# Six stores instead of five leave out one DMA engine, in 26 pieces each, and V gets a sixth buffer

## The chip, the cores and the metric

The kernel runs on one core of a Trainium2 chip. A core has five engines that work at the same time and meet through semaphores: TensorE (PE; its weight loads are listed as PEld), VectorE (DVE), ScalarE (ACT), GpSimd (POOL) and SyncE (SP). Sixteen DMA engines move data between the chip's main memory (DRAM) and the on-chip memory (SBUF, 128 partitions). Any of SP, ACT and POOL can issue a transfer; each has its own queue on every one of the sixteen engines.

The metric is the device time of one execution in microseconds (us). The kernel before takes 1285.98 us, the median of three runs (1284.94 to 1286.35).

## The reference

It is attention for one query row per head, with its gradients. There are 2 x 32 = 64 heads; each has a K and a V of 8192 rows by 128, in bfloat16.

```python
def _fwd_reference(q, k, v):
    scale = q.shape[-1] ** -0.5
    scores = jnp.einsum("bhqd,bhkd->bhqk", q, k) * scale
    p = _softmax(scores, axis=-1)
    return jnp.einsum("bhqk,bhkd->bhqd", p, v)

def reference(q, k, v, grad_out):
    ...
    _out, _vjp = jax.vjp(_f, q, k, v)
    _grads = _vjp(grad_out)
    ...
    return (_out0, *[jnp.asarray(_g) for _g in _grads])
```

So the kernel returns the output (64 x 128), the gradient of q (64 x 128), and the gradients of K and V, which are as large as K and V: 64 x 8192 x 128 each. K and V are 268 MB together and are read once; their gradients are 268 MB and are written once. The gradient of K is, in each head, an outer product of a column of weights `dS` with the row q, that of V an outer product of the weights `P` with the row of grad_out.

## The kernel before

**Tiles.** One K or V of a head is a tile of 128 partitions x 64 x 128 (2 MB, 16 KB in each partition). `load(h)` takes one buffer `kt` and one `vt` from a pool of `UNITS = 5` each and has SP load K and then V (L104). The gradients are written over K and V in the same buffers: `outer` (L271, DVE) puts the gradient of V into `vt` and that of K into `kt`, and `store` (L331, ACT) writes a buffer out. A buffer is free for the next load when its store has landed.

**Stages.** An iteration `h` of the main loop has eight steps `j`, each in two halves. PE transposes K (`j` 0 to 3) and V (`j` 4 to 7) of head `h` by a product with the identity (L113); ACT, in two places DVE, copies the result out of PSUM (`ev`, L120 and L118); PE multiplies it by the column of q or grad_out (L136). Beside it the head before, `p = h - 1`, is finished: sums, weights, the products with `rows` (L241), and the eight `outer`. The V gradient of `p` is stored at `j = 4`, the K gradient at `j = 7`; both issues stand in ACT's instruction stream among its copies. At the end of iteration `h`, `load(h + 3)` is issued by SP. Heads 0 to 4 are loaded at the start. The last head's two gradients are stored in halves.

**The order around the change.** The order on each engine is written out (`manual_schedule`); waits are put in by the framework. Two of its habits matter. First, the transfers of SP and ACT take turns on eight semaphores, in the order of the program, and the transfers of POOL on another eight: a transfer waits on its issuing engine until the one eight places earlier has landed. In an ordinary head four transfers of SP and ACT are issued (store V, store K, load K, load V), so that each waits for its own kind of two heads earlier. Secondly, a pool hands out its buffers in the order in which the planner expects them to be free, not strictly in turn.

**The stores in pieces.** `store` hands every 26th of the 128 gradients (`(2 * h + w) % RARE == RARE // 2 - 1`; `w` 0 is V, 1 is K) to `store_by_fifteen`. Those are numbers 12, 38, 64, 90 and 116: the V gradients of heads 6, 19, 32, 45 and 58. `store_by_fifteen` writes the 128 partitions in 24 pieces (L299) with POOL, not ACT. Partitions 16 to 19 and 48 to 51, which the code calls `fifth`, go out in four pieces of two. Between the pieces stand 11 transfers `turn(n)` (L285): four bytes twice from each of `n` rows of q, into a tile `spare` that nobody reads. Pieces and turns are laid in such an order that, as the function's name says, fifteen of the sixteen DMA engines carry the data. So POOL issues 35 transfers for one such store, and ACT none. The pieces of four partitions with `size=16384` go out as rows of 16 KB, the others as two packets of 8 KB a row.

Of the kernel before, what the change touches and what calls it, by code (L numbers as in the profile page):

```python
# [11 lines left out]
BF16 = mybir.dt.bfloat16  # L12
# [3 lines left out]
HC = CH // 2  # L16
QG = 4
OG = 4
RARE = 26
UNITS = 5  # L20


@with_exitstack
def kernel(
# [11 lines left out]
    nc = tc.nc  # L36
    B, H, Sq, D = q.shape
    Sk = k.shape[2]
    P = nc.NUM_PARTITIONS
    assert Sq == 1 and D == P  # L40
    BH = B * H
    NT = Sk // P
# [5 lines left out]
    const = ctx.enter_context(tc.tile_pool(name="const", bufs=1))  # L48
# [17 lines left out]

    kvp = ctx.enter_context(tc.tile_pool(name="kv", bufs=UNITS))
    evp = ctx.enter_context(tc.tile_pool(name="ev", bufs=5))
# [28 lines left out]
    def load(h):  # L97
        x = heads[h]
        x.kv = [
            kvp.tile([P, NT, D], BF16, name="kt", tag="kt"),  # L100
            kvp.tile([P, NT, D], BF16, name="vt", tag="vt"),
        ]
        for dst, src in zip(x.kv, (k_v, v_v)):
            nc.sync.dma_start(out=dst[:], in_=src[h])  # L104
# [173 lines left out]
    turns = []  # L278

    def turn(n):  # L280

        i = 4 * len(turns)
        turns.append(n)
        two = lambda t: t.rearrange("p (a b) -> p a b", a=2)
        nc.gpsimd.dma_start(  # L285
            out=two(spare[0:n, :])[:, :, i : i + 2], in_=two(q_rows[0:n, :])[:, :, 0:2]
        )

    def store_by_fifteen(h, w):

        dst, src = (dv_v, dk_v)[w][h], heads[h].kv[1 - w]

        def rows(lo, n, step=4, size=8192):
            own = slice(lo, lo + step * (n - 1) + 1, step)
            nc.gpsimd.dma_start(out=dst[own], in_=src[own], max_dma_last_dim=size)  # L299

        def fifth(r):
            rows(16 + r, 2, step=32)

        for r in range(4):

            if r == 1:
                fifth(r)
                turn(14)
            rows(52 + r, 11)
            rows(r, 4, size=16384)  # L310
            if r == 0:
                fifth(r)
                turn(3)
            elif r == 3:
                turn(10)
                fifth(r)
                turn(9)
            else:
                turn(5)
            rows(20 + r, 3)  # L320
            if r == 2:
                fifth(r)
                turn(14)
            rows(96 + r, 8)
            rows(32 + r, 4, size=16384)
            turn(5)

    def store(h, w, a=0, b=NT):
        if (2 * h + w) % RARE == RARE // 2 - 1:
            return store_by_fifteen(h, w)  # L330
        nc.scalar.dma_start(out=(dv_v, dk_v)[w][h][:, a:b, :], in_=heads[h].kv[1 - w][:, a:b, :])  # L331

    def outer_and_store(h, w, i):

        outer(h, w, i)
        if h == BH - 1 and i % 2:
            store(h, w, (i - 1) * CH, (i + 1) * CH)


    spare = const.tile([16, 1024], BF16)  # L340
    turn(5)
    nat = const.tile([BH, 2, D], BF16)
    for i, src in enumerate((q_rows, do_rows)):
# [9 lines left out]
    with tc.manual_schedule():  # L353
        for h in range(min(UNITS, BH)):
            load(h)
        for h in range(BH + 1):
# [4 lines left out]
            for j in range(NS):  # L361
# [24 lines left out]
                if x and p < BH - 1 and j in (4, 7):  # L386
                    store(p, j // 7)
# [7 lines left out]
                if j == 7:  # L395
                    if x and UNITS <= h + 3 < BH:
                        load(h + 3)
                    if y and h % QG == 0:
                        spread_rows(h // QG)
        for w, dst in enumerate((o_rows, dq_rows)):  # L400
            tps = ps_tp.tile([BH, P], BF16, name="tps", tag="tp")
            nc.tensor.transpose(tps[:], colsT[:, w, :], ident_bf[:])
            rows = const.tile([BH, D], BF16, name=f"rows{w}")
# [33 lines left out]
```

## Time and profile before

| | us |
|---|---|
| median of three runs (1284.94 to 1286.35) | 1285.98 |
| the profiled execution | 1286.92 |
| its span, first to last instruction | 1285.1 |
| PE, ACT, DVE busy | 1060.3, 909.3, 883.8 |
| POOL busy | 105.8 |

The profile is of one execution. Its page gives the busy time of each engine, then the span in 40 equal slices of 32 us (busy tenths of each engine, the share that the DMA engines were busy, and the GB/s that they moved), the DMA queues, and groups of instructions with what ended the idle time ahead of them. In these views, q1 is SP's queue (loads), q10 is ACT's (stores), q0 is POOL's (the pieces and turns), and q8 fetches instructions. The trace holds more than the views print: a record of every DMA packet, with its queue, start, duration and size, but not the number of the engine that moved it.

| packets of | size | count | usual ns of one |
|---|---|---|---|
| loads, q1 | 16 KB | 16384 | 611 |
| stores, q10 | 16 KB | 15488 | 611 |
| pieces, q0 | 16 KB | 160 | 611 |
| pieces, q0 | 8 KB | 960 | 309 |
| instruction fetches, q8 | 16 KB | 148 | 943 (mean) |

### The profile page before, as it was taken

How to read it: one execution, taken by the hardware profiler on the slowest of the kernel's cores; microseconds unless marked ns; L12 is line 12 of the kernel's file. 1: busy time of each engine (PE TensorE's matmuls, PEld its weight loads, DVE VectorE, ACT ScalarE, POOL GpSimd, SP SyncE). 2: the span in 40 equal slices, each digit the busy share in tenths (PEclk: the TensorE clock that was granted, in tenths of full speed). 3: DMA queues.
4: the chain of work that ended last, by engine and by line, in shares of the span. 5: the costliest groups of instructions: out<-in, count | busy, mean ns of one | idle time of the engine just before them, and what ended most of it. 6: DMA issues, size and time to landing. Idle time of an engine off the chain costs nothing.

```text
span 1285.1 us, 42433 instructions
## 1 busy us (share of the span) xinstructions
PE 1060.3 (83%) x18948; PEld 877.3 (68%) x18948; DVE 883.8 (69%) x1511; ACT 909.3 (71%) x1043; POOL 105.8 (8%) x193
## 2 busy tenths in 40 slices
PE   5999888848998799499997984999889849899983
PEld 4777777637777677477776774777767737777772
DVE  1887777737787486378875773787767636778775
ACT  5877778737887586488875774877767736788771
POOL 1000111000002110000021200000111000001120
PEclk9999999969999697799996897998979877999996
DMA  9999999999999999999999999999999999999998
GB/s 396 418 426 428 426 426 425 423 431 427 426 426 426 413 424 427 423 427 425 428 426 399 427 426 418 428 427 428 419 403 426 425 419 391 428 429 425 425 424 336
DMA packets 43879, 539.69 MB, mean 420 GB/s; under 512 B 10192, under 2 KB 10192, under 8 KB 10192
## 3 DMA queue, kind: packets, MB, share of 16 engines
q1 hardware_dynamic: 18432, 268.44, 49.5%
q10 hardware_dynamic: 18320, 258.02, 47.4%
q0 software_dynamic: 6944, 10.51, 2.2%
q8 instruction: 148, 2.42, 0.7%
q14 instruction: 35, 0.29, 0.1%
HBM read 268.47 MB, written 268.47 MB: 418 GB/s over the span
## 4 chain that ended last, share of the span: by engine, by line
PE 40%; DMA 26%; ACT 19%; DVE 11%; issue 3%; ACTq 0%; DVEq 0%; SPq 0%
PE tp L113 23%; ACT ev L120 18%; DMA vt<-in_v_dram 9%; DVE ev L118 9%; DMA out_dram<-vt 9%; PE acc L241 9%; DMA kt<-in_k_dram 4%; PE sm L136 4%; DMA out_dram<-kt 3%; PE dp L206 1%; PE dp L136 1%; PE c L259 1%; DMA nat<-in_grad_out_dram 1%; ACT E_f L175 1%; PE sm L170 1%
## 5 line engine op out<-in xcount | busy, mean ns | idle before, releaser
L120 ACT CAST ev<-tp 128x1024 bf16<-128x1024 f32 x896 | 881.2, 1024 | 335.7 <-PE tp L113 232.3
L113 PE MATMUL tp<-ident_bf,vt 128*128 128x128 bf16 x4096 | 327.4, 225 | 134.7 <-ACT ev L120 121.6
L113 PEld LDWEIGHTS <-vt 128*128 128x128 bf16 x4096 | 268.9, 100 | 167.3 <-issue 153.2
L113 PE MATMUL tp<-ident_bf,kt 128*128 128x128 bf16 x4096 | 335.9, 228 | 17.2 <-DMA kt<-in_k_dram 6.5
L113 PEld LDWEIGHTS <-kt 128*128 128x128 bf16 x4096 | 249.4, 101 | 131.5 <-issue 123.2
L136 PEld LDWEIGHTS <-ev 128*128 128x128 bf16 x8192 | 324.4, 98 | 2.2 <-issue 0.2
L271 DVE TENSOR_TENSOR kt<-qd,dS 128x2048 bf16<-128x2048 bf16 x256 | 310.0, 1212 | 0.0
L271 DVE TENSOR_TENSOR vt<-qd,P 128x2048 bf16<-128x2048 bf16 x256 | 295.8, 1216 | 0.0
L118 DVE CAST ev<-tp 128x1024 bf16<-128x1024 f32 x128 | 156.7, 1224 | 186.4 <-PE tp L113 179.4
L136 PE MATMUL dp<-doT_all,ev 128*128 128x1 bf16 x4096 | 178.5, 164 | 0.1
L136 PE MATMUL sm<-qT_all,ev 128*128 128x1 bf16 x4096 | 176.0, 164 | 0.0
L299 POOL DMA_DIRECT2D out_dram<-vt x120 | 67.0, 560 | 1032.7 <-DVE vt L271 832.1
L241 PE MATMUL acc<-vt,wz 128*32 128x512 bf16 x1024 | 109.3, 418 | 17.8 <-DVE wz L186 17.8
L241 PE MATMUL acc<-kt,wz 128*32 128x512 bf16 x1024 | 103.4, 396 | 0.1
L172 DVE TENSOR_SCALAR negm<-sm 128x1 f32<-128x1 f32 x64 | 9.8, 154 | 108.8 <-PE sm L170 108.8
L241 PEld LDWEIGHTS <-wz 128*32 128x32 bf16 x2048 | 52.8, 93 | 32.1 <-DVE wz L186 22.7
L285 POOL DMA_DIRECT2D spare<-in_q_dram x57 | 34.1, 598 | 121.1 <-DMA out_dram<-vt 107.0
L206 PE MATMUL dp<-ld,ones_f 128*128 128x2 f32 x128 | 25.8, 271 | 21.0 <-DVE ld L193 20.9
L206 PEld LDWEIGHTS dp<-ld,ones_f 128*128 128x128 f32 x128 | 20.6, 202 | 31.1 <-DVE ld L193 31.0
L160 DVE TENSOR_REDUCE mp<-sm 128x1 f32<-128x64 f32 x64 | 14.4, 225 | 36.9 <-PE sm L136 36.9
L211 DVE RECIPROCAL rl_all<-dp 128x1 f32<-128x1 f32 x64 | 10.7, 168 | 32.0 <-PE dp L206 32.0
L170 PE MATMUL sm<-gm,ones_f 1*128 1x1 f32 x128 | 25.8, 268 | 0.0
(42 smaller groups left out, 310.5 us busy)
## 6 DMA issues: line engine op xcount, KB each, us to landing
kt<-in_k_dram SPq DMA_DIRECT2D x64, 2048.0 KB, 22.9
vt<-in_v_dram SPq DMA_DIRECT2D x64, 2048.0 KB, 31.5
out_dram<-kt ACTq DMA_DIRECT2D x63, 2048.0 KB, 26.9
out_dram<-vt ACTq DMA_DIRECT2D x58, 2048.0 KB, 21.9
out_dram<-vt POOLq DMA_DIRECT2D x20, 176.0 KB, 23.2
out_dram<-vt POOLq DMA_DIRECT2D x40, 64.0 KB, 23.0
out_dram<-vt POOLq DMA_DIRECT2D x20, 128.0 KB, 22.6
out_dram<-vt ACTq DMA_DIRECT2D x2, 1024.0 KB, 10.9
```

Source lines behind the costliest of these rows:

```text
L113: nc.tensor.matmul(tp[:, i, :], lhsT=x.kv[w][:, n, :], rhs=ident_bf[:], start=True, stop=True)
L118: nc.vector.tensor_copy(out=ev[:], in_=tp[:])
L120: nc.scalar.copy(out=ev[:], in_=tp[:])
L136: nc.tensor.matmul((x.dp if w else x.sm)[:, n : n + 1], lhsT=ev[:, i, :], rhs=col, start=True, stop=True,)
L160: nc.vector.reduce_max(out=x.mp[:], in_=x.sm[:, 0:NT], axis=AX.X)
L170: nc.tensor.matmul(mb, lhsT=ones_f[0:1, :], rhs=x.gm[:], start=True, stop=True)
L175: nc.scalar.activation(out=x.E[:], in_=x.sm[:, 0:NT], func=ACT.Exp, bias=negm[:], scale=scale, accum_out=x.ld[:, 0:1],)
L206: nc.tensor.matmul(x.lsum, lhsT=ones_f[:], rhs=x.ld[:], start=True, stop=True)
L241: nc.tensor.matmul(acc[32 * g : 32 * g + 32, :], lhsT=wz[w][k][:, n // 4, :], rhs=rows[:, n : n + 4, :].rearrange("p n d -> p (n d)"), sta ...
L271: nc.vector.tensor_tensor(out=x.kv[1 - w][:, n : n + CH, :].rearrange("p n (d t) -> p n d t", t=2), in0=row.unsqueeze(1).to_broadcast([P, ...
L285: nc.gpsimd.dma_start(out=two(spare[0:n, :])[:, :, i : i + 2], in_=two(q_rows[0:n, :])[:, :, 0:2])
L299: nc.gpsimd.dma_start(out=dst[own], in_=src[own], max_dma_last_dim=size)
```

## The change

- `RARE` is 22 and the condition `(2 * h + w) % RARE == 6`: numbers 6, 28, 50, 72, 94 and 116, so the V gradients of heads 3, 14, 25, 36, 47 and 58 are stored in pieces, six instead of five.
- Each such store is now 26 transfers. One, the partitions 0, 4, 8 and 12, is issued by ACT, where the whole store stood before. POOL issues 18 pieces and 7 turns: a piece of 44 partitions (52 to 95) in place of four of 11, the `fifth` partitions as 48 to 51 and as 16 to 19 in place of four pairs, and the rest as before.
- V has six buffers (`V_UNITS`), K keeps five.
- `spare` has half the width, and `turn` begins again at its start after 64 turns.

```diff
-RARE = 26
+RARE = 22
 UNITS = 5
+V_UNITS = 6
...
-            kvp.tile([P, NT, D], BF16, name="vt", tag="vt"),
+            kvp.tile([P, NT, D], BF16, name="vt", tag="vt", bufs=V_UNITS),
...
-        i = 4 * len(turns)
+        i = 4 * len(turns) % 256
...
-        def rows(lo, n, step=4, size=8192):
+        def rows(lo, n, step, size=8192, eng=nc.gpsimd):
             own = slice(lo, lo + step * (n - 1) + 1, step)
-            nc.gpsimd.dma_start(out=dst[own], in_=src[own], max_dma_last_dim=size)
-
-        def fifth(r):
-            rows(16 + r, 2, step=32)
-
+            eng.dma_start(out=dst[own], in_=src[own], max_dma_last_dim=size)
+
+        rows(0, 4, 4, 16384, nc.scalar)
+
+        rows(52, 44, 1)
+        turn(5)
         for r in range(4):
-
-            if r == 1:
-                fifth(r)
-                turn(14)
-            rows(52 + r, 11)
-            rows(r, 4, size=16384)
-            if r == 0:
-                fifth(r)
-                turn(3)
-            elif r == 3:
-                turn(10)
-                fifth(r)
-                turn(9)
-            else:
-                turn(5)
-            rows(20 + r, 3)
+            if r == 3:
+                rows(16, 4, 1)
+                turn(12)
+            rows(20 + r, 3, 4)
             if r == 2:
-                fifth(r)
-                turn(14)
-            rows(96 + r, 8)
-            rows(32 + r, 4, size=16384)
+                rows(48, 4, 1)
+                turn(12)
+            rows(96 + r, 8, 4)
             turn(5)
+            for lo in (r, 32 + r)[r == 0 :]:
+                rows(lo, 4, 4, 16384)
 
     def store(h, w, a=0, b=NT):
-        if (2 * h + w) % RARE == RARE // 2 - 1:
+        if (2 * h + w) % RARE == 6:
             return store_by_fifteen(h, w)
...
-    spare = const.tile([16, 1024], BF16)
+    spare = const.tile([16, 512], BF16)
```

## The prediction

> **What bounds the kernel now.** I read the slices first, then the queues, then windows, waits and the timeline.
>
> ```profile
> PE 1060.3 (83%) x18948; PEld 877.3 (68%) x18948; DVE 883.8 (69%) x1511; ACT 909.3 (71%) x1043; POOL 105.8 (8%) x193
> ...
> DMA  9999999999999999999999999999999999999998
> GB/s 396 418 426 428 426 426 425 423 431 427 426 426 426 413 424 427 423 427 425 428 426 399 427 426 418 428 427 428 419 403 426 425 419 391 428 429 425 425 424 336
> ...
> q1 hardware_dynamic: 18432, 268.44, 49.5%
> q10 hardware_dynamic: 18320, 258.02, 47.4%
> q0 software_dynamic: 6944, 10.51, 2.2%
> ```
>
> No compute engine is full; the DMA engines are, in every slice. The queues' shares add up to 100.1% with the two small ones. So the question is which of the sixteen engines has most to do.
>
> No view says that, but the packet records do: on one engine each packet starts 4 ns before the last one ends, so packets can be strung into sixteen chains. A row of 16 KB takes 611 ns (607 from start to start), except on one engine, where the mean is 639 (635). That engine's chain holds one 8 KB piece of 960, so it is the engine that the stores in pieces leave out, and one instruction fetch of 148. Its extra time goes with PE's instructions: in 260 to 270, 520 to 530 and 1040 to 1050 us, where PE stands still, all slow packets together have 0.01 to 0.02 us over 611, otherwise about 0.48 in 10 us. I call it the fifth. Its work: 2048 rows less 5 x 8, 2008 x 0.635 = 1275.1 us; some 620 packets of 4 and 8 bytes at 6 ns, 3.7; others 0.8; with a start at about 2 us that is 1282. Followed from 30 to 1268 us its chain has no pause but nine of one packet's length, where I take a record to be missing, and some 4 us of short ones; it ends at 1282.2. Each of the others: 30760 rows / 15 x 0.607 = 1244.8; fetches, 148 x 1.36 (0.94, and 0.42 that the packet behind loses) / 15 = 13.4; 4.5 of small ones: 1262.7. They have some 19 us to spare, and lose them here:
>
> ```profile
> 300.00:380.00 80.00, 72.61 (x1362) 59.86 (x1359) 64.38 (x111) 64.64 (x74) 0.00 (x0) 1.00 1.01 427
> 420.00:430.00 10.00, 5.81 (x76) 5.59 (x76) 2.12 (x3) 5.27 (x7) 2.41 (x5) 0.50 0.97 378
> 520.00:540.00 20.00, 5.19 (x69) 4.98 (x69) 1.87 (x4) 5.27 (x7) 0.00 (x0) 0.59 1.01 421
> 670.00:690.00 20.00, 11.61 (x193) 10.46 (x191) 8.71 (x11) 10.18 (x12) 3.99 (x7) 0.68 0.96 383
> 780.00:800.00 20.00, 5.32 (x71) 5.10 (x71) 1.63 (x3) 5.27 (x7) 0.00 (x0) 0.58 1.01 414
> 940.00:950.00 10.00, 6.28 (x86) 5.94 (x85) 2.62 (x4) 5.75 (x8) 1.97 (x4) 0.50 0.96 374
> 1040.00:1060.00 20.00, 4.81 (x46) 4.60 (x46) 1.71 (x4) 4.26 (x6) 0.00 (x0) 0.56 1.01 412
> 1070.00:1090.00 20.00, 18.24 (x323) 14.79 (x320) 14.38 (x25) 15.28 (x18) 0.00 (x0) 0.92 0.94 374
> ```
>
> The last column is GB/s: 427 in a quiet stretch, 374 to 421 in dips. Taken as (427 - x)/427 of each, the seven dips are 1.1, 0.3, 2.1, 0.6, 1.2, 0.7 and 2.5: 8.5 us. Their origin is in the waits and the timeline:
>
> ```profile
> ACT ev L120 <- DMA vt<-in_v_dram: 63.9, 4, 17.3
> ...
> 414.28 1.02 ACT L120 CAST ev<-tp 128x1024 bf16<-128x1024 f32 x1
> 420.28 0.33 SPq L104 DMA_DIRECT2D kt<-in_k_dram  x1
> 420.70 0.41 SPq L104 DMA_DIRECT2D vt<-in_v_dram  x1
> 422.69 0.34 ACTq L331 DMA_DIRECT2D out_dram<-vt  x1
> 423.13 1.01 ACT L120 CAST ev<-tp 128x1024 bf16<-128x1024 f32 x1 [7.83 <-issue]
> ```
>
> ACT stands from 415.3 to 422.7 at the issue of a store, and the copies behind it stand too, with PE behind them. A store in pieces takes none of the eight semaphores of SP and ACT, so the turns slip by one: the next V store (head 20) waits for the K load of head 22, issued 400.0, landed 422.6. About five heads later the order slips again, and V store 25 waits for V load 27. Those are the pauses of 8 and of 15 to 17 us.
>
> **The change, part by part.** The sum is made against the profiled execution, 1286.92 us (span 1285.1 and 1.8 around it); the median of the runs is 0.94 less, and I move it by the same difference.
>
> *A sixth store in pieces.* The fifth loses 8 rows, 8 x 0.635 = -5.1 us. Each of fifteen gains 8/15 of a row, +0.3, and has 19 to spare. Nothing in the trace excludes that a row costs the fifth only the common 0.607, which makes it -4.9.
>
> *26 transfers for 35.* POOL issues 152 in all for 177, at 0.56 us each, in 1032 us of idle time: 0. Small packets fall from 5824 to about 4740 (one per transfer and engine, and 52.5 per turn), at 6 ns and a sixteenth of them on each engine: -0.4. POOL's piece waits for the transfer eight places ahead (landing 22 to 23 us), so a store lasts about 17/8 x 22.6 + 22.6 = 71 us, where 27/8 x 22.6 + 22.6 = 99 stood. Of the 44-partition piece no row shows the landing; between 22.6, the rows of other pieces, and 35 (the slowest median of a 2 MB load is 31.5) the buffer is kept 12 us longer at most, which the sixth buffer covers.
>
> The 44-partition piece leaves out the fifth only if it is dealt to eleven engines, four rows each. The Trainium skill, "DMA: Bandwidth & Descriptors", section on why a semaphore rises by 16, says that the count of engines is the largest number up to 16 that divides the slowest dimension, 11 here, from a cursor that moves on. No run here shows a piece of 44; by that rule, this term stays as it is.
>
> *One piece by ACT.* It stands where the store stood and costs the same issue, 0.34 us, six times instead of none, against 335.7 us in which ACT waits before L120: 0. It takes a semaphore's turn, so the slip is gone: by the built order, V store 4 waits for V store 2, as all do between.
>
> *Six V buffers.* V loads no longer wait behind the store in pieces, or (SP's 211.6 us on V stores) ask for a neighbour's buffer. The pauses of 8 to 17 us go. What comes late next is the load itself: a head takes ACT and PE 17.3 us (from exponential to exponential) and the fifth 32 x 0.635 = 20.3, so PE will wait some 3 us in each head. For the time this is 0, not the 8.5 us of the dips: the fifth was never idle in them. Ends: 0 and -8.5; I take 0, the row nearest (its chain).
>
> *The end.* Last of all at 1283.2 was not the fifth but another engine, 1.0 us later. Engines met in the dip of 1070 to 1090, where even the fifth's queue was nearly empty; without it the others run ahead. Ends: -1.0 and, if that engine stays, +5.5; I count 0. And compute: the last loads leave the turns of V store 60 with K load 62. That load landed at 1218.8, the store went out at 1218.2, the last store at 1272.7, and its packets on engines without a queue ran to 1276.1, 3.4 later. So the end by compute is 1218.8 + 57.9 = 1276.7, exactly where the fifth ends by my sum: no cover is left, and each us that K load 62 lands later counts. Ends -1 and +3; I take 0.
>
> Sum: -5.1 - 0.4 = -5.5; fifth to 1276.7; profiled 1281.4, median 1280.5 us.
>
> **The rivals.** (1) *Another engine sets the end.* At the end nine engines still had work beyond 1276.5, and the one at 1283.2 is not relieved. It comes so if the others lose their 19 us elsewhere: 1286.0 + 0.3 - 0.4 = 1285.9. For it speaks that chain; against it, that it was idle in the dips.
>
> (2) *The dips were the price.* If the fifth's short pauses hide starvation, the dips are gained too: 1280.5 - 8.5 = 1272.0 at most, 1276.3 for half. Against it: 31 to 32 rows in each 20 us of the fifth's chain, in dips and outside.
>
> (3) *Slower: PE waits in every head and its clock falls.* The granted clock was 0.5 for 3 to 31 us behind the pauses, and heads then took 20.5 us (426.2 to 446.7). If the small waits keep it there, from head 12 (237.9) on 51 heads take 20.5: 1283 for the last exponential, 16.2 to the last store, 3.4 and the rest: about 1305. It decides once more than nine tenths of the heads run at half clock, for the fifth needs 20.3 itself. Against it: pauses of 1.3 to 2.2 us (231, 241, 763, 1013) brought 3 to 10 us of half clock, no more.
>
> (4) *The pieces miss their engines.* Did the 44-partition piece reach all sixteen, the fifth would get back about 3 of its 8 rows: 1282.4.
>
> (5) *The engine spared is not the slow one.* Then eight rows leave an engine that has 19 us to spare: 1285.9. Against it: the slow chain is the one without pieces, and it is as slow in 300 to 380 us, without POOL's traffic, as beside it. The Trainium skill, same page, "Latency and other measured facts", calls engines 7 and 15 usually slower and guesses at POOL's descriptor rings; by that rule this rival would hold, and the trace does not agree.
>
> **How the numbers follow.** Under 0.2% (2.6 us) a measurement of this kernel tells no change from one. My forecast, with the end moved by up to 3 us, 0.55; (1) 0.19; (2) 0.05; (3) 0.08; (4) 0.05; (5) 0.03; other losses, such as a late K load 62 beyond 10 us, 0.05. Faster: 0.55 + 0.05 + 0.05 and a small part of (1), 0.67; same: 0.22; slower, (3) and half of the last: 0.11. The likeliest case alone spans 1278.5 to 1283.4; the range reaches up to (1) and a little beyond, and down to half of (2): 1277.5 to 1287.
>
> **What would show it.** Right: a span near 1279.6; fifth's chain with 2000 rows and still without pauses; no ACT issue held for more than 3 us before V store 60; no GB/s dip below 415 between the first and last slices; PE waits on loads, some 3 us a head; small packets near 4740. Wrong: the fifth ends early and another engine after it; PE's granted clock at half for most heads; PE waiting on V store 60 beyond 1219 us; SP held by POOL's semaphores.

## The result: 0.65% slower, and where the profile shows it

The changed kernel takes 1295.62 us, the median of six runs (1290.88 to 1299.1); the kernel before took 1286.43 beside it. The ratio is 1.0065, with a 95% interval of 1.0037 to 1.0094. The forecast was 1280.5. The profiled execution of the changed kernel took 1295.18 us, with a span of 1293.4, against 1286.92 and 1285.1 before.

The page after, in its busy times, granted clock and bandwidth by slice, and its chain of work that ended last:

```profile
PE 1099.0 (85%) x18948; PEld 902.8 (70%) x18948; DVE 884.1 (68%) x1511; ACT 907.3 (70%) x1043; POOL 92.3 (7%) x168
...
PEclk9999999898898997889888897897999878889977
DMA  9999999999999999999999999999999999999986
GB/s 396 419 427 427 417 428 427 426 427 426 423 427 427 428 427 427 420 424 424 428 428 426 428 411 412 422 426 426 424 425 408 418 421 425 426 426 422 407 359 276
...
DMA kt<-in_k_dram 59%; PE tp L114 10%; DMA out_dram<-kt 10%; ACT ev L121 7%; PE acc L242 4%; DVE ev L119 3%; PE sm L137 2%; DMA nat<-in_grad_out_dram 1%; PE dp L207 1%; PE dp L137 1%; DVE kt L272 0%; ACT E_f L176 0%; DVE vt L272 0%; PE c L260 0%; PE sm L165 0%
```

In the middle the lowest slice has 408 GB/s where 391 stood (the prediction had asked for none below 415), but the last two slices have 359 and 276 where 424 and 336 stood. The chain that ended last is loads of K. Four of the windows that showed the pauses before, in the changed kernel:

```profile
420.00:430.00 10.00, 8.59 (x175) 7.67 (x171) 6.88 (x11) 8.55 (x11) 0.00 (x0) 1.00 1.01 429
...
670.00:690.00 20.00, 16.77 (x293) 13.68 (x293) 13.67 (x24) 13.87 (x16) 0.00 (x0) 0.91 1.01 427
...
940.00:950.00 10.00, 9.58 (x175) 8.05 (x172) 7.66 (x10) 8.63 (x10) 0.00 (x0) 0.90 1.00 423
...
1070.00:1090.00 20.00, 16.77 (x270) 13.55 (x268) 12.51 (x22) 12.72 (x15) 0.00 (x0) 0.83 1.01 426
```

378, 383, 374 and 374 GB/s have become 429, 427, 423 and 426. The waits of the changed kernel agree: PE's transposes wait on K loads 36 times, at most 6 us, and ACT's 64 us behind V loads are 2.6. Before V store 60 the trace puts no pause of ACT above 2.4 us down to the issue of a store.

```profile
PE tp L114 <- DMA kt<-in_k_dram: 75.3, 36, 6.0
...
ACT ev L121 <- DMA vt<-in_v_dram: 2.6, 1, 2.6
```

So the middle went as forecast and the end did not. The same two windows, before and then after (the last columns are PE's clock, the busy share of the DMA engines, and GB/s):

```profile
30.00:1180.00 1150.00, 966.68 (x17324) 800.41 (x17323) 806.23 (x1376) 829.32 (x950) 79.75 (x140) 0.92 1.00 423
1180.00:1260.00 80.00, 71.73 (x1331) 59.61 (x1327) 61.92 (x104) 64.18 (x75) 20.36 (x36) 0.98 1.01 425
```

```profile
30.00:1180.00 1150.00, 997.37 (x17304) 819.06 (x17303) 805.58 (x1377) 825.97 (x949) 71.75 (x125) 0.90 1.01 424
1180.00:1260.00 80.00, 65.97 (x1095) 54.74 (x1094) 50.34 (x83) 52.74 (x61) 14.98 (x26) 0.83 0.94 389
```

The packet records give the account. By 1180 us the changed kernel had moved as many bytes as the kernel before would have moved 2.9 us later, and its sixteen engines had stood idle for 1.4 us each instead of 4.3 (a stretch less a sixteenth of all packet time in it, each packet counted without the 4 ns by which it overlaps the next). From 1180 us to the last data packet, at 1291.6 us, they stood 14.4 us; before, 4.5, up to 1283.1. That is 2.9 won and 9.9 lost; the remaining 1.5 of the 8.5 between the two ends is slower transfer, above all in 1180 to 1220, where a row of a load took 649 ns in the mean against 613 before.

The reason is in the transfers' times from issue to landing, from the pages before and after:

```profile
kt<-in_k_dram SPq DMA_DIRECT2D x64, 2048.0 KB, 22.9
vt<-in_v_dram SPq DMA_DIRECT2D x64, 2048.0 KB, 31.5
out_dram<-kt ACTq DMA_DIRECT2D x63, 2048.0 KB, 26.9
```

```profile
kt<-in_k_dram SPq DMA_DIRECT2D x64, 2048.0 KB, 36.9
vt<-in_v_dram SPq DMA_DIRECT2D x64, 2048.0 KB, 39.5
out_dram<-kt ACTq DMA_DIRECT2D x63, 2048.0 KB, 22.3
```

The loads now queue for 37 to 40 us and the stores are short. In both kernels the two queues move alike while both have work (198 and 199 GB/s in 1210 to 1220 us before, 196 and 208 after), so a long load queue stays long. The Trainium skill, "DMA: Bandwidth & Descriptors", section "Queues, rings and completion order", says that an engine takes turns between the queues that have work, packet by packet; these numbers agree. A pause of PE is what changes the balance: the stores run dry and the loads catch up (run e5, below, shows this). At the end it matters. Before, the last V load landed at 1249.9 us and enough stores were waiting to fill the engines behind it; after, it landed at 1259.3, and in 1260 to 1270 us 5.8 engines of 16 were busy, because the stores had not been computed yet.

And ACT was held once, by the one semaphore turn that the prediction had named. The changed kernel's timeline of ACT (start, length, engine):

```profile
1221.11 4.11 ACT L121 CAST ev<-tp 128x1024 bf16<-128x1024 f32 x4
1230.84 0.34 ACTq L322 DMA_DIRECT2D out_dram<-vt  x1
1231.27 1.93 ACT L121 CAST ev<-tp 128x1024 bf16<-128x1024 f32 x2 [6.06 <-issue]
```

V store 60 went out when K load 62 had landed, 1230.8 us; this is the wait beyond 1219 us that the prediction had listed as a sign of being wrong. From there to the end PE waited for no load, so in this execution the end follows from that hold and the compute behind it. PE's clock was at half right behind it (the third last column):

```profile
1231.00:1246.00 15.00, 13.43 (x168) 11.28 (x167) 7.55 (x17) 8.51 (x11) 2.84 (x5) 0.51 0.93 389
```

The exponentials of heads 60 and 63 (first and last start), before and after:

```profile
L175 ACT ACTIVATE E_f<-sm,negm x4: 364/365/365, 1202.7 to 1256.5; 128x64 f32<-128x64 f32 x4
```

```profile
L176 ACT ACTIVATE E_f<-sm,negm x4: 320/364/365, 1209.7 to 1271.9; 128x64 f32<-128x64 f32 x4
```

The last exponential is 15.4 us later, and the span follows it by 21.5.

### The profile page after: what moved, and what is told of

The parts are those of the page before. It is cut to its first block, busy times and chain, and to the rows that moved or that the text cites. A ratio compares the mean times of both kernels' runs of the same rounds, so it can differ in the third digit from the quotient of the medians.

```text
span 1293.4 us, 42438 instructions
## 1 busy us (share of the span) xinstructions
PE 1099.0 (85%) x18948; PEld 902.8 (70%) x18948; DVE 884.1 (68%) x1511; ACT 907.3 (70%) x1043; POOL 92.3 (7%) x168
## 4 chain that ended last, share of the span: by engine, by line
DMA 70%; PE 17%; ACT 7%; DVE 4%; issue 2%; ACTq 0%; SPq 0%; DVEq 0%
DMA kt<-in_k_dram 59%; PE tp L114 10%; DMA out_dram<-kt 10%; ACT ev L121 7%; PE acc L242 4%; DVE ev L119 3%; PE sm L137 2%; DMA nat<-in_grad_out_dram 1%; PE dp L207 1%; PE dp L137 1%; DVE kt L272 0%; ACT E_f L176 0%; DVE vt L272 0%; PE c L260 0%; PE sm L165 0%
## 5 line engine op out<-in xcount | busy, mean ns | idle before, releaser
L114 PE MATMUL tp<-ident_bf,kt 128*128 128x128 bf16 x4096 | 370.6, 243 | 81.6 <-DMA kt<-in_k_dram 75.3
L114 PEld LDWEIGHTS <-kt 128*128 128x128 bf16 x4096 | 273.9, 109 | 213.4 <-issue 132.4
L114 PE MATMUL tp<-ident_bf,vt 128*128 128x128 bf16 x4096 | 317.3, 221 | 65.7 <-ACT ev L121 45.2
L137 PEld LDWEIGHTS <-ev 128*128 128x128 bf16 x8192 | 331.1, 99 | 2.2 <-issue 0.2
L114 PEld LDWEIGHTS <-vt 128*128 128x128 bf16 x4096 | 260.8, 98 | 99.8 <-issue 75.1
L300 POOL DMA_DIRECT2D out_dram<-vt x108 | 61.9, 576 | 1018.6 <-DVE vt L272 866.3
L242 PE MATMUL acc<-vt,wz 128*32 128x512 bf16 x1024 | 124.3, 476 | 7.6 <-DVE wz L187 7.3
L161 DVE TENSOR_REDUCE mp<-sm 128x1 f32<-128x64 f32 x64 | 14.4, 224 | 65.7 <-PE sm L137 65.7
L207 PEld LDWEIGHTS dp<-ld,ones_f 128*128 128x128 f32 x128 | 24.0, 234 | 19.3 <-DVE ld L194 18.9
L286 POOL DMA_DIRECT2D spare<-in_q_dram x44 | 26.0, 590 | 130.6 <-DMA out_dram<-vt 130.5
L155 ACT CAST qd<-pb 128x1024 bf16<-128x1024 f32 x16 | 16.2, 1012 | 12.3 <-PE pb L147 11.6
## 6 DMA issues: line engine op xcount, KB each, us to landing
out_dram<-vt POOLq DMA_DIRECT2D x6, 704.0 KB, 16.3
```

The lines of the kernel that those rows point to most:

```text
L114: nc.tensor.matmul(tp[:, i, :], lhsT=x.kv[w][:, n, :], rhs=ident_bf[:], start=True, stop=True)
L137: nc.tensor.matmul((x.dp if w else x.sm)[:, n : n + 1], lhsT=ev[:, i, :], rhs=col, start=True, stop=True,)
L155: nc.scalar.copy(out=qd[:], in_=pb[:])
L161: nc.vector.reduce_max(out=x.mp[:], in_=x.sm[:, 0:NT], axis=AX.X)
L207: nc.tensor.matmul(x.lsum, lhsT=ones_f[:], rhs=x.ld[:], start=True, stop=True)
L242: nc.tensor.matmul(acc[32 * g : 32 * g + 32, :], lhsT=wz[w][k][:, n // 4, :], rhs=rows[:, n : n + 4, :].rearrange("p n d -> p (n d)"), sta ...
```

## The experiments

The theories that the expectations speak of: A, the loads are late at the end since no pause lets them run ahead; B, the sixth buffer by itself; C, the new pieces or the sixth store; D, the last hold of ACT; E, the end is the later of compute and the fifth's work; F, the fifth engine alone; G, all sixteen engines end nearly together. The runs were made in several rounds, each with the kernel before beside it, whose median was 1286.1 to 1287.0; the ratios are against that one. Each table row has the median and ratio with its interval, then from the profiled execution the exponentials of heads 60 and 63, and the mean idle time of the sixteen engines in 20 to 1180 us and from 1180 us to the last data packet.

| run | us | ratio to before | head 60, head 63 | idle |
|---|---|---|---|---|
| before | 1286.4 | | 1202.7, 1256.5 | 4.3, 4.5 |
| after | 1295.6 | 1.0065 [1.0037, 1.0094] | 1209.7, 1271.9 | 1.4, 14.4 |
| e1 before, six V | 1294.5 | 1.0063 [1.0047, 1.0080] | 1213.1, 1271.0 | 3.9, 14.7 |
| e2 after, five V | 1296.8 | 1.0085 [1.0067, 1.0104] | 1217.6, 1273.9 | 3.0, 13.9 |
| e3 after, no piece by ACT | 1295.9 | 1.0071 [1.0051, 1.0090] | 1216.9, 1274.9 | 4.4, 16.7 |
| e5 after, one slip | 1290.1 | 1.0037 [1.0023, 1.0052] | 1200.1, 1268.5 | 2.7, 11.5 |
| h2 after, five stores | 1295.4 | 1.0057 [1.0040, 1.0073] | 1211.2, 1272.4 | 1.8, 14.5 |
| i1 before, six V, turns kept | 1290.6 | 1.0029 [1.0010, 1.0048] | 1211.0, 1271.6 | 1.6, 13.0 |
| f1 after, tail by SP | 1290.2 | 1.0019 [1.0003, 1.0036] | 1213.7, 1268.6 | 2.3, 10.9 |
| f2 e3, last slip and hold out | 1288.7 | 1.0017 [1.0008, 1.0027] | 1199.4, 1261.4 | 4.0, 6.7 |
| f3 e1, last slip and hold out | 1285.2 | 0.9993 [0.9984, 1.0002] | 1199.2, 1257.4 | 3.6, 6.6 |
| f4 e5, tail by SP | 1287.3 | 1.0006 [0.9995, 1.0017] | 1198.7, 1260.1 | 2.8, 9.3 |
| g1 f2, last loads first | 1289.1 | 1.0014 [1.0001, 1.0027] | 1199.0, 1255.6 | 4.1, 7.1 |
| g2 after, last loads first | 1291.2 | 1.0030 [1.0017, 1.0043] | 1211.7, 1264.4 | 2.2, 8.2 |
| g3 f3, last loads first | 1285.4 | 0.9983 [0.9969, 0.9998] | 1198.2, 1252.5 | 4.0, 6.3 |
| h4 e5, last loads first | 1289.0 | 1.0016 [1.0006, 1.0026] | 1201.9, 1254.8 | 2.9, 8.2 |
| g4 before, four stores | 1289.7 | 1.0013 [0.9995, 1.0030] | 1206.8, 1260.2 | 6.1, 5.4 |
| h1 before, six stores | 1285.6 | 0.9985 [0.9974, 0.9995] | 1204.1, 1257.9 | 2.5, 4.7 |
| h3 g3, six old stores | 1287.5 | 0.9998 [0.9985, 1.0011] | 1197.6, 1252.7 | 2.9, 6.5 |
| i2 f3, six old stores | 1286.8 | 0.9995 [0.9973, 1.0016] | 1196.9, 1255.5 | 3.1, 6.6 |

### Which part of the change: the buffer, the turns or the pieces

e1, the kernel before with six V buffers (and the narrower `spare`, for room):

```diff
+V_UNITS = 6
...
-            kvp.tile([P, NT, D], BF16, name="vt", tag="vt"),
+            kvp.tile([P, NT, D], BF16, name="vt", tag="vt", bufs=V_UNITS),
```

> The kernel before with six V buffers and nothing else of the change (the scratch tile that the turns write is cut to 512 columns to make room, as in the change). Theory A, late loads: in the changed kernel no pause lets the loads run ahead, so the load queue stays about 40 us long, the store queue short, the last V load lands at 1259.3 instead of 1249.9 us, and the DMA engines have too few stores left to be filled after it. Here the semaphore turns still slip (V store 20 waits for K load 22), so the pauses stay and the time stays near the kernel before, 1283 to 1289 us. Theory B, the sixth V buffer itself delays the K loads: 1292 to 1297 us, K loads landing near 40 us after issue up to the end. Theory C, the new cutting into pieces and the sixth such store cost the time: unchanged, 1286 us.

1294.5 us, so B by the number, but not by its mechanism: K loads landed 21.0 us after issue (median), sooner than before. What had changed was the kind of the slip. By the built order V store 59, behind the last store in pieces, now waits for V load 61; in the kernel before it waits for K load 61, which lands some 10 us sooner. The timeline of ACT in e1:

```profile
1190.73 5.12 ACT L121 CAST ev<-tp 128x1024 bf16<-128x1024 f32 x5 [0.75 <-PE tp L114]
1209.57 0.37 ACTq L332 DMA_DIRECT2D out_dram<-vt  x1
1210.04 1.93 ACT L121 CAST ev<-tp 128x1024 bf16<-128x1024 f32 x2 [14.18 <-DMA vt<-in_v_dram]
```

ACT stood 14.2 us and head 60's exponential came 37.3 us behind head 59's. In the kernel before the same store went out unheld at 1198.98.

e2, the changed kernel with five V buffers:

```diff
-V_UNITS = 6
+V_UNITS = 5
```

> The changed kernel with five V buffers. Theory A, late loads: the turns still do not slip, so ACT is held nowhere for 8 us; what pauses there are come from V loads that wait behind a store in pieces. If these are under 5 us the end stays near 1291 to 1297 us; if pauses of 8 us and more return, the loads run ahead and the end comes back to 1283 to 1288 us. Theory B, the sixth buffer: 1283 to 1288 us with no long pause. Theory C, the pieces: 1295 us, unchanged.

1296.8 us. The pauses came back (heads 16, 27, 38, 49 and 60 took 31 to 35 us), for with five buffers the turns slip again in spite of ACT's piece: V store 59 went out at 1214.1 us, when V load 61 had landed. But one of them lay at head 60, so A's forecast for this case, 1283 to 1288, was wrong: a pause near the end is a loss, whatever it did earlier.

e3, the changed kernel with ACT's piece given to POOL:

```diff
-        rows(0, 4, 4, 16384, nc.scalar)
+        rows(0, 4, 4, 16384)
```

> The changed kernel with ScalarE's piece of each store in pieces given to POOL like the others, so that such a store takes no semaphore turn and the turns slip again; six V buffers and six stores stay. Theory A, late loads: the pauses of 8 us and more come back, the last V load lands at 1250 us or earlier, the end at 1279 to 1288 us. Theories B and C: the pauses cost what they cost before or nothing, the time stays at 1293 to 1299 us.

1295.9 us with the pauses back, the last one again at head 60 (37.6 us). The last V load landed at 1249.2, as theory A had wanted, and it did not help. So theory A alone was not enough, and theory D was formed: the hold that comes last counts.

i1, the kernel before with six V buffers and the turns kept, without new pieces or a sixth store:

```diff
+        t = const.tile([1, 2], BF16, name=f"t{h}")
+        nc.scalar.dma_start(out=t[:], in_=q_rows[0:1, 0:2])
```

> The kernel before with six V buffers and, at each of its five stores in pieces, one transfer of 4 bytes issued by ACT to take the semaphore turn that the store leaves out: no slip, as in the change, but the old 35 pieces and five stores. Theory A: the turns and the sixth buffer together make the changed kernel's long load queue and its late end, so this has no pause of 8 us or more, K loads that land some 40 us after issue and 1292 to 1298 us, as the changed kernel. If the new pieces or the sixth store were needed for it: 1284 to 1289 us.

1290.6 us, between the two. Its profiled execution, 1295.16 us, was the longest of its ten, and shows the changed kernel's picture: no head over 24.5 us, loads of 34.8 and 40.2 us, 392 GB/s in 1180 to 1260:

```profile
30.00:1180.00 1150.00, 997.15 (x17284) 818.30 (x17283) 804.23 (x1375) 824.44 (x948) 79.63 (x140) 0.90 1.01 424
1180.00:1260.00 80.00, 68.50 (x1116) 56.42 (x1114) 51.78 (x85) 53.84 (x63) 20.45 (x36) 0.83 0.95 392
```

So buffers and kept turns suffice for the late end, and are slower than before by 0.1 to 0.5%. By the medians that is 4.2 of the 9.2 us; the intervals of i1 and the changed kernel overlap a little.

h2, the changed kernel with five stores in pieces:

```diff
-RARE = 22
+RARE = 26
...
-        if (2 * h + w) % RARE == 6:
+        if (2 * h + w) % RARE == 12:
```

> The changed kernel with five stores in pieces (heads 6, 19, 32, 45, 58) instead of six, each in the new 26 transfers with ScalarE's piece, six V buffers. The end is as in the changed kernel: loads that land some 40 us after issue and V store 60 waiting for K load 62. Theories A and D: 1291 to 1298 us, the fifth plays no part. If the sixth store or its pieces cost the time: 1286 to 1289 us.

1295.4 us, as the changed kernel. The sixth store plays no part there. h2 differs from i1 in the new pieces alone, ACT's among them (i1 has a 4-byte transfer in its place), and is 4.8 us slower by the medians. Two more pairs, below, differ in the pieces alone in the same way, and the new pieces are slower in both: f2 than i2 by 1.9 and g1 than h3 by 1.7. So the new pieces seem to cost some 2 to 5 us. Why is not settled: no run looks into it. The price does not simply add to that of the late end, for f4, below, has the new pieces and wins back 8.3 of the 9.2 us.

### The hold at the end

The stores of heads 60 to 63 issued by SP, which then has no load left to issue, so that a store that waits its turn holds no copy:

```diff
-        nc.scalar.dma_start(out=(dv_v, dk_v)[w][h][:, a:b, :], in_=heads[h].kv[1 - w][:, a:b, :])
+        eng = nc.sync if h > 59 else nc.scalar
+        eng.dma_start(out=(dv_v, dk_v)[w][h][:, a:b, :], in_=heads[h].kv[1 - w][:, a:b, :])
```

f1 is that alone, on the changed kernel.

> The changed kernel with the stores of heads 60 to 63 issued by SP, which has no load left by then, so that a store that waits for its semaphore's turn (V store 60 for K load 62, landed 1230.8 us) holds no copy on ACT. Theory D, the hold at the end: ACT stood until 1230.8 at V store 60, head 61's exponential came at 1234.3; without the hold the last exponential is bound by the last K load alone, 1249.2 + 16.3 (as in the kernel before, 1240.2 to 1256.5) = 1265.5 instead of 1271.9, and the time falls by some 6 us to 1286 to 1291. Theory A, late loads alone: the loads are as late as they were or later, since stores go out sooner and share the engines: 1292 to 1296 us.

1290.2 us, 5.4 less by the medians, in D's range. Single executions went from 1285.9 to 1296.2, and the profiled one was the longest.

f2 is e3 with this and with ACT's piece kept in the last store in pieces (`nc.scalar if h == 58 else nc.gpsimd`), so that V store 59 waits for no load.

> The run with all pieces on POOL (1295.9 us), but ScalarE's piece kept in the last store in pieces (head 58), and the stores of heads 60 to 63 issued by SP. Its pauses behind the first five stores in pieces stay, the hold at the end (V store 59 waiting for V load 61, a pause of 20 us before head 60's exponential) goes. Theory D, only the hold that comes last counts: the last exponential moves from 1274.9 to 1258 to 1263 and the time to 1280 to 1287 us. If the pieces or the sum of all pauses cost the time: 1293 to 1296 us.

1288.7 us, 7.2 less than e3; four pauses of 39 to 42 us stayed, behind heads 14, 25, 36 and 47, the fifth went. D gave 1280 to 1287, so the direction is right and the end a little later than it said. f3 does the same to e1, with a 4-byte transfer by ACT at head 58:

```diff
+        if h == 58:
+            t = const.tile([1, 2], BF16)
+            nc.scalar.dma_start(out=t[:], in_=q_rows[0:1, 0:2])
```

> The kernel before with six V buffers (1294.5 us as run), with one transfer of 4 bytes issued by ACT beside the last store in pieces (head 58) to take the semaphore turn that this store leaves out, and the stores of heads 60 to 63 issued by SP. Theory D: the pause of 20 us before head 60's exponential goes, the last exponential moves from 1271.0 to 1256 to 1262 and the time to 1280 to 1287 us. Theory B, the sixth buffer delays by itself: 1292 to 1296 us.

1285.2 us, 9.2 less than e1, in D's range. The last exponential in e1 and in f3:

```profile
L176 ACT ACTIVATE E_f<-sm,negm x4: 321/361/361, 1213.1 to 1271.0; 128x64 f32<-128x64 f32 x4
```

```profile
L176 ACT ACTIVATE E_f<-sm,negm x4: 364/365/367, 1199.2 to 1257.4; 128x64 f32<-128x64 f32 x4
```

Head 60 moved by 13.9 us and head 63 by 13.6. Three earlier pauses of 37 to 38 us (heads 21, 34, 47) are still in f3 and it is no slower than the kernel before. So a sixth buffer does not delay by itself, and an early pause costs little; the last one decided.

e5 adds a pause to the changed kernel, by giving ACT's piece to POOL in the store of head 47 alone:

```diff
-        rows(0, 4, 4, 16384, nc.scalar)
+        rows(0, 4, 4, 16384, nc.gpsimd if h == 47 else nc.scalar)
```

> The changed kernel with ScalarE's piece given to POOL in one store alone, that of head 47, so that the turns slip once, late: from head 49 on a V store waits for the K load two heads ahead. Theory A, late loads: one pause of 5 to 10 us near 990 to 1010 us, behind it K loads land ahead, the last V load at 1250 us or earlier, and the end comes at 1282 to 1290 us although a pause was added. If the kernel is instead short of time on PE (its clock at half in short windows), a pause added makes it slower: 1297 to 1303 us. Theories B and C: 1295 us, unchanged.

1290.1 us: a pause of some 14 us added (head 49 took 31.0) and 5.5 us taken off, 0.1 above A's range. Head 60 came at 1200.1 instead of 1209.7. In this one execution the state of the queues can be seen on both sides of the pause. K loads, issued in 760 to 960 us and then in 1015 to 1205 us:

```profile
kt<-in_k_dram SPq DMA_DIRECT2D x10, 2048.0 KB, 38.1
```

```profile
kt<-in_k_dram SPq DMA_DIRECT2D x10, 2048.0 KB, 22.0
```

Between them, in 985 to 995 us, the loads moved 389 GB/s by the packet records and the stores of ACT nothing. So one pause took some 16 us off the load queue, and they stayed off up to K load 62 (24.0 us from issue to landing, 36.7 in the changed kernel). Then V store 60 was held for K load 62 (head 61 took 29.6). f4 takes that hold out by SP:

> The changed kernel with one slip at the store of head 47 (1290.1 us as run, exponential of head 60 at 1200.1, then 29.6 us to the next) and the stores of heads 60 to 63 issued by SP. Theory D and A together: the hold of V store 60 until 1226.1 goes, the last exponential is bound by K load 63, 1246.4 + 16.3 = 1262.7 or a little later instead of 1268.5: 1283 to 1287 us, 3 to 8 less than in the run beside it without a slip. Theory A alone, without D: 1289 to 1291 us.

1287.3 us, 2.8 less, just above the 1283 to 1287 that D and A gave. Pause and release together make up 8.3 of the 9.2 us that the change cost.

### What a sixth store in pieces is worth

g4 takes one store in pieces from the kernel before (that of head 6); h1 has six, in the old pieces and spaced as in the change:

```diff
-        if (2 * h + w) % RARE == RARE // 2 - 1:
+        if (2 * h + w) % RARE == RARE // 2 - 1 and h > 6:
```

> The kernel before with four stores in pieces instead of five: that of head 6 goes by ACT whole; all later slips stay as they were. Theory F, the prediction's: in the kernel before the fifth engine sets the end, so 8 rows more on it cost 8 x 0.635 = 5.1 us: 1290 to 1292.5 us. If compute behind the last loads sets it: 1284.5 to 1287.5 us.

```diff
-RARE = 26
+RARE = 22
...
-        if (2 * h + w) % RARE == RARE // 2 - 1:
+        if (2 * h + w) % RARE == 6:
```

> The kernel before with a sixth store in pieces, all in its old 35 transfers, spaced as in the change (heads 3, 14, 25, 36, 47, 58), five V buffers, nothing by ACT (the columns that the turns write are used in rotation, as in the change). The turns slip as in the kernel before, behind head 58 by a K load (V store 59 for K load 61), the last long pause comes at the store of head 53 or 54. Theory F, the fifth engine sets the end: 5.1 us off, 1279.5 to 1282.5 us. Theory G, by now all sixteen engines are loaded alike, each pause makes the loads run alone for a while and costs about 1 us on each engine, so what the fifth gains is lost by the others: 1284 to 1288 us.

g4 is 3.3 us slower by the medians, between its two ranges, and not clear of noise (ratio from 0.9995 to 1.0030). h1 is faster by 0.15%, 0.05 to 0.26, which is 0.6 to 3.3 us, and not by 5.1. So theory F is too simple and G describes h1. In the records of the kernel before the engine that ended last, at 1283.1 us, is not the fifth; engines end between 1276 and 1283. h1 moved that last end to 1282.0.

The sixth store in f3, where nothing is held at the end (i2, the edit of h1):

> The run with six V buffers, five old stores in pieces, the last slip taken out and the stores of heads 60 to 63 by SP (1285.2 us), with a sixth store in the old pieces. Fifth engine alone at the end (theory F): 5.1 us off, 1279.5 to 1281.5 us. Theory G, all engines end nearly together and an added slip costs each about 1 us: 1283.5 to 1287 us.

1286.8 us against f3's 1285.2: in G's range, and no gain at all. Where each such store slips to a V load, as here, it brings one pause more (four against three), and the mean idle time behind 1180 us is the same. The same step from g3 gives h3:

> The run with five stores in pieces and the last loads first (1285.4 us) with a sixth store, in the old 35 transfers. It stands beside the run with six in the new transfers (1289.1 us). Theory G: six instead of five add a pause, about 1 us on each engine: 1285 to 1288 us. If the new transfers were what cost 3.7 us there, and the fifth sets the end here: 1280 to 1283 us. If the sixth store costs it whatever its pieces: 1288 to 1290 us.

1287.5 against g3's 1285.4, in G's range again.

### The last loads first

The stores of head 59 too are issued by SP, behind the last V load (the same edit with `h > 58`, and `store(59, ...)` moved behind `load(63)`). g1, g3 and h4 are f2, f3 and f4 with it, g2 is the changed kernel with it.

> The run of before with all pieces on POOL but the last ones (1288.7 us: six V buffers, six stores in pieces, no hold behind the last), with the stores of head 59 too issued by SP, behind the last V load, so that the last loads share the engines with no later store. Theory E: the end is the later of two, the fifth engine's work (six stores in pieces: 1276.7 us by the prediction's sum) and the compute behind the last loads. Here the last loads land before 1236 instead of 1245.6, the last exponential comes at 1248 to 1256 instead of 1261.4, its last store is issued 16 later and lands 4 after that, so compute ends by 1276 and the fifth sets the end: 1278 to 1282 us, faster than both kernels. If the fifth's work is worth nothing even then, or the end is bound elsewhere: 1284 to 1289 us.

> The changed kernel with the stores of heads 59 to 63 issued by SP behind the last V load, and nothing else. Theory A with E: the last loads land some 20 us earlier (1259.3 becomes about 1235), heads 61 to 63 then follow head 60 (exponential at 1209.7) at 17.3 us each, the last exponential at 1262 instead of 1271.9, the last store out 16 later and landed after 4 more: 1282 to 1286 us, 10 to 13 less than the changed kernel. If the loads' lateness is not what sets the end: 1291 to 1296 us.

> The kernel before with six V buffers, the transfer of 4 bytes beside the last store in pieces, and the stores of heads 59 to 63 issued by SP behind the last V load. Theory E: with five stores in pieces the fifth's work ends at 1282.0, so although compute ends earlier than in the run without this (1285.2 us) the time stays: 1283.5 to 1286 us, and the run with six stores beside it is 3 to 6 us faster. If the fifth does not set it, both are alike.

> The changed kernel with one slip, at the store of head 47, and the stores of heads 59 to 63 issued by SP behind the last V load: one pause instead of five, compute a little ahead of the loads at the end, the last loads first. In the run without the last step (1287.3 us) the engines stood 2.8 us up to 1180 and 9.3 behind 1230. Theory E: the last exponential comes at 1250 to 1256 instead of 1260.1, the idle time behind 1230 falls to about 5 us, and the time to 1281 to 1285 us, faster than both kernels. If the share of the loads in the last stretch costs as much as it gains (both runs of this step showed bandwidth of 346 to 403 GB/s in 1200 to 1220 us, when few stores run): 1286 to 1289 us.

Theory E fell. g1 and h4, which were to beat both kernels, did not; g3's own time met its range, but the run with six stores beside it is 3.7 us slower instead of 3 to 6 faster. g1 brought the last V load to 1236.3 and the last exponential to 1255.6, as expected, and the time stayed, 1289.1 against 1288.7. Its windows:

```profile
1180.00:1200.00 20.00, 16.61 (x315) 13.98 (x312) 14.94 (x25) 15.07 (x20) 1.68 (x3) 1.00 1.01 421
1200.00:1220.00 20.00, 16.14 (x273) 12.96 (x274) 12.49 (x22) 12.99 (x14) 5.22 (x9) 0.83 0.93 374
1220.00:1270.00 50.00, 39.12 (x698) 30.43 (x698) 39.52 (x67) 30.98 (x38) 3.40 (x6) 0.94 1.01 423
```

The engines are full in 1220 to 1270 now, but 374 GB/s stand in 1200 to 1220, where f2 had 424: the last loads still waited for buffers (K load 63 went out at 1215.5), and the stores of head 59 stood behind them. That the two belong together is argued from the order on SP. h4 shows the same (331 GB/s in 1200 to 1210 us) and is 1.7 us slower than f4. g2 is faster than the changed kernel by 4.4 us, less than the 10 to 13 expected, and its 1291.2 us lies in the range that was given for loads that do not set the end; its last exponential came at 1264.4, 2.4 later than foreseen, but its engines still stood 8.2 us behind 1180. So the lateness of the last loads alone is not the whole of the late end.

No run is faster than the kernel before by the 0.2% that the prediction took as the least that can be told: g3 and h1 are the best, by 0.17 and 0.15%, with intervals that end just below 1 (0.9998 and 0.9995).

## Why the prediction was wrong

**What held.** The slip is gone from V store 4 on, with the pauses of 8 to 17 us and the dips. PE waits on K loads in more than half of the heads, by 2.1 us in the mean of 36 waits (some 3 in each were forecast). The chain that I take for the fifth's could be followed from 29.5 to 1262 us without a pause, at 639.6 ns a row. A store in pieces took 66 to 74 us between its first and last data packet (71 forecast). Rival 3, half the clock in every head, did not come: the clock is 0.898, 0.916 before. Of rival 2, the dips as a price, 2.9 us came true in the middle, where the sum had 0; the late end hid them. For rival 4, pieces that reach the fifth, an 8 KB packet there should last about 639 / 611 x 309 = 323 ns; 11 of 1152 lie in 312 to 335 ns, 15 of 960 before, so there is no sign of it. Small packets of POOL were 5176, not 4740, and the 44-partition piece landed after 16.3 us (median), outside my bounds of 22.6 to 35; both are small. So is a slip in its reading of the queues: their shares add up to 99.9%, not 100.1.

**The step that failed** is *The end*: "So the end by compute is 1218.8 + 57.9 = 1276.7, exactly where the fifth ends by my sum: no cover is left, and each us that K load 62 lands later counts. Ends -1 and +3; I take 0." The rule came near and its input was wrong. K load 62 landed at 1230.8, so the rule gives 1288.7; the last data packet ended at 1291.6, 14.9 later than the forecast, and the span followed. I had read 1218.8 from a trace with pauses and kept it for a kernel without them. In that trace the load held nothing: V store 60 went out at 1218.2, with ACT busy right up to it, so the 57.9 us were compute alone. Behind a real hold they grew by the 2.9 us that the rule misses: head 62 took 20.3 us instead of 17.3, at half the clock (0.51 in 1231 to 1246 us). The +3 at the upper end had no reason from a row.

**Where it came from** is one step earlier, *Six V buffers*: "PE will wait some 3 us in each head. For the time this is 0, not the 8.5 us of the dips". It is 0 as long as the engines are full, and in 30 to 1180 us they were. But a PE that waits for each load has no lead, and what it has not computed the stores can't send; at the end that is 14.4 us of idle engines instead of 4.5. In the kernel before, heads 54 to 60 ran at 17.3 to 18.1 us behind the pause at head 52, and had that lead at the end; in e5, where a pause was put in, heads 50 to 57 did the same behind it. I named this way of failing (K load 62 more than 10 us late) and gave it 0.05.

**The mis-sized term.** *A sixth store in pieces* was put at -5.1 us. Alone it measured -0.6 to -3.3 (h1). That lies between the term and rival 1, in which another engine sets the end and nothing is gained (-0.1); that h1's 1285.6 is near that rival's 1285.9 is luck, for the kernel before took 1287.0 beside h1. In the changed kernel the term is worth nothing, as compute sets its end (h2). Behind it stands a wrong reading: the other fifteen engines did not have 19 us to spare. All packet times of the kernel before, less the 4 ns of overlap, are 1272.3 us for each of the sixteen in the mean, so 1271.8 for the fifteen where the sum had 1262.7. The sum allowed 148 packets some 0.4 us each behind the fetches; 366 rows took over 0.25 us longer than 611 ns. What those more are waiting for is open. Some 8 us to spare, and less with every pause, is what theory G describes.

**The new pieces** were put at 0 and seem to cost 2 to 5 us; this is open.

## What to carry to other kernels

A stall in the middle of a stream that is full is not a cost yet, and taking it away is not a gain: ask what the stall did to the queues, and above all how far the loads are ahead when the last one is issued. Cost the end of a kernel from the state that the change will leave, not from the landing times of the trace before; the last load's landing, the compute behind it and the stores that are left to cover it belong in the sum. Where transfers take turns on a few semaphores, see for the last ones which transfer each of them waits for, and on which engine that wait stands.

## What the runs showed that was not expected

- One transfer of 4 bytes that takes a semaphore's turn, with the last stores issued by another engine, was worth 9.2 us (e1 to f3).
- Two regimes: where the last exponential came at 1268 us or later, the span ended 21 to 22 us after it in seven of eight runs (f1: 25.8); where it came by 1262 us, the span was 1283.6 to 1289.0 us whatever it was (1252.5 to 1261.4). g2 lies between (1264.4, span 1288.9).
- Some kernels scatter much more between executions than others, and it is open why: after 1290.9 to 1299.1, h2 1289.2 to 1299.0, f1 1285.9 to 1296.2, against 2.6 us in f3 and 2.8 in h1. The lack of pauses does not explain it, for the kernel before, which has them, ran from 1284.6 to 1295.3. The Trainium skill, "TensorE: Matmul & The Clock Gate", section "HAM oscillation", describes PE falling to half its clock when the wait for each tile's transfer is longer than a window of about 3.4 us. The runs do not bear it out as the cause of the scatter: PE's 36 waits on K loads in the changed kernel are shorter in the mean (2.1 us), and while the two longest of its six executions have its lowest granted clock (0.892, the others 0.898 to 0.901), f1's longest has f1's highest, 0.906. In that one the packets were slower: 1277.9 us of packet time for each engine, against 1269.7 to 1275.0 in the other profiled executions.
